# Layer-norm head of a fused attention and feed-forward kernel: loads on one queue, rstd on GpSimd, more normalising on ScalarE

## The chip, the cores and the metric

One core of a Trainium2 chip runs the whole program. The metric is the device time of one execution in microseconds, taken as the median of several runs. Engines are called PE (TensorE), DVE (VectorE), ACT (ScalarE), POOL (GpSimd) and SP (SyncE); PEld is PE's weight load.

## The reference, cut to what matters

```python
x = A_x                                   # (1, 2048, 576), bf16
xn = _layernorm(x, axis=-1)               # (x - mean) / sqrt(var + 1e-5)
return x + _A_ref(xn, A_wqkv, A_wo) + _B_ref(xn, B_w_gate, B_w_up, B_w_down)

# A: linear attention, 32 heads of 18
qkv = xn @ wqkv                           # phi(t) = where(t > 0, t + 1, exp(t)) + 1e-6
kv = einsum(phi(k), v); z = sum(phi(k))   # over the 2048 rows
o = (phi(q) @ kv) / (phi(q) . z + 1e-6); return o @ wo
# B: (gelu(xn @ w_gate) * (xn @ w_up)) @ w_down, hidden width 4608
```

The variance enters as rstd = (var + 1e-5) to the power -0.5, one number per row.

## The kernel before

The 2048 rows are 16 tiles of 128 (`NS`), the 576 columns of x five chunks of 128 (`KT`, the last one half full). The program has a first stage of some 57 us (layer norm, the k and q products, their activation phi, and an accumulated product of xn with phi(k) called G), a short passage to about 67 us, and then four rounds of the feed-forward part with the attention output added in.

Per tile n the first stage does this:

- statistics of the two halves of x (`ln_half`, L211, DVE) and their aggregate, mean and variance (`ln_aggr`, L214, DVE);
- rstd as exp(-0.5 ln(var + eps)), two one-column instructions on ACT (`ln_rstd`, L218 and L219);
- the normalised tile xn: on DVE (`ln_norm`, L232) for tiles 0 and 1, in two pieces each, and for even tiles after that; on ACT (`ln_norm_act`, L227) for odd tiles from 3 on, with a bias -mean*rstd made by POOL (`ln_bias`, L222);
- the transpose xnT: for tiles 0 and 1 by five PE transposes (L247) into PSUM and two copies (`tp_copy`, L251), for the others by a DMA transpose on SP's queue (L254);
- four groups of five matmuls, two halves of k and two of q (`kq_mm`, L262), each followed by an exp on ACT (L269) and a combining instruction on DVE (`kq_phi`, L274);
- seven matmuls of G (L293), which read xn and phi(k), and one POOL addition for z (`z_add`, L197).

The order on every engine is written out by a small planner. Each piece of work is a `step` with an engine, a length, a rank, the steps that it follows and, for loads, a time from which its data is taken to be there (`X_AT`, `W_AT`). `in_order` walks through the steps, takes the engine that can begin first and on it the lowest rank, and so makes one list; the instructions are issued in that list's order, and each engine runs its own in order. The lengths are the planner's reckoning only; waits at run time are on semaphores.

Ahead of the planned steps the loads are issued, in this order (`load_x` is L93, `load_w` L107 and L108; `load_w(1)` are the k weights, `load_w(0)` the q weights):

```python
load_x(0, 1)
load_x(1, 1, nc.scalar)
nc.scalar.preload_act_table_set("natural_log_exp_and_others")
load_w(1)
load_x(2, 2)
load_w(0)
load_x(4, 4)
```

PE meanwhile runs 38 matmuls on an identity (`spin`, L132), and POOL makes the identity and fills constant columns (L171 to L175), then the block mask `bmask` (L179 to L184), one chunk of `g_sb` (L189) and `ones` (L192). The mask is read when kv is masked, `g_sb` and `ones` in the passage after the first stage.

Of the kernel before, what the change touches and what calls it, by code (L numbers as in the profile page):

```python
# [8 lines left out]
ACT = mybir.ActivationFunctionType  # L9
ALU = mybir.AluOpType  # L10
BF16 = mybir.dt.bfloat16
F32 = mybir.dt.float32
# [3 lines left out]
P = 128  # L16
HP = 64
S = 2048
D = 576
H = 32  # L20
DH = 18
F = 4608
NS = S // P
# [5 lines left out]
KT = 5  # L29
# [4 lines left out]
EPS_LN = 1e-5  # L34
# [23 lines left out]
def kernel(  # L58
# [11 lines left out]
    nc = tc.nc  # L70
# [8 lines left out]
    const = ctx.enter_context(tc.tile_pool(name="const", bufs=1))  # L79
# [10 lines left out]
    x_sb = persist.tile([P, NS, D], BF16, name="x_sb")  # L90

    def load_x(n0, cnt, on=nc.sync):
        on.dma_start(x_sb[:, n0:n0 + cnt, :], x_view[:, n0:n0 + cnt, :])  # L93
# [14 lines left out]
        nc.sync.dma_start(wqkv_sb[0:HP, 4, c], A_wqkv[512:576, c])  # L108

    load_x(0, 1)  # L110
    load_x(1, 1, nc.scalar)
    nc.scalar.preload_act_table_set("natural_log_exp_and_others")
    load_w(1)
    load_x(2, 2)
# [4 lines left out]

    ident = const.tile([P, P], BF16, name="ident")  # L120
    make_identity(nc, ident[:])
    eps_ln = const.tile([P, 1], F32, name="eps_ln")
    nc.vector.memset(eps_ln[:], EPS_LN)
    eps_att = const.tile([P, 1], F32, name="eps_att")
    nc.vector.memset(eps_att[:], EPS_ATT)
    neg1 = const.tile([P, 1], F32, name="neg1")
    nc.vector.memset(neg1[:], -1.0)

    def spin(count):

        for _ in range(count):
            nc.tensor.matmul(ps_all[:, 7, 0:P], lhsT=ident[:], rhs=ident[:], start=True, stop=True)  # L132
# [19 lines left out]
    def load_gu(i, part):  # L152
# [17 lines left out]
    xn = apool.tile([P, NS, XW], BF16, name="xn")  # L170
# [4 lines left out]
    nc.gpsimd.memset(pk[:, :, D + 1:D + 2], 1.0)  # L175

    bmask = const.tile([P, CR], F32, name="bmask")
    bm3 = bmask[:].rearrange("p (h e) -> p h e", e=DH)
    nc.gpsimd.memset(bmask[:], 1.0)  # L179
    nc.gpsimd.affine_select(  # L180
        out=bm3, in_=bm3, compare_op=ALU.is_ge, fill=0.0,
        base=0, pattern=[[-DH, 7], [0, DH]], channel_multiplier=1,
    )
    nc.gpsimd.affine_select(  # L184
        out=bm3, in_=bm3, compare_op=ALU.is_ge, fill=0.0,
        base=DH - 1, pattern=[[DH, 7], [0, DH]], channel_multiplier=-1,
    )
    g_sb = apool.tile([P, KT, D], BF16, name="g_sb")
    nc.gpsimd.memset(g_sb[:, 4, :], 0.0)  # L189

    ones = const.tile([P, P], BF16, name="ones")
    nc.gpsimd.memset(ones[:], 1.0)  # L192
    z_sum = apool.tile([P, D], F32, name="z_sum")
    z_bf = apool.tile([P, D], BF16, name="z_bf")

# [6 lines left out]
    mv = persist.tile([P, NS, nc.vector.BN_AGGR_DIM], F32, name="mv")  # L202
    rstd = persist.tile([P, NS], F32, name="rstd")
    nbias = persist.tile([P, NS], F32, name="nbias")
# [3 lines left out]
    def ln_half(n, h):  # L208
        if h == 0:
            ln_raw[n] = asmall.tile([P, 2, nc.vector.BN_STATS_DIM], F32, name="stats")  # L210
        nc.vector.bn_stats(out=ln_raw[n][:, h, :], in_=x_sb[:, n, h * HALF:(h + 1) * HALF])  # L211

    def ln_aggr(n):
        nc.vector.bn_aggr(out=mv[:, n, :], in_=ln_raw[n][:])  # L214

    def ln_rstd(n):
        r = rstd[:, n:n + 1]
        nc.scalar.activation(out=r, in_=mv[:, n, 1:2], func=ACT.Ln, bias=eps_ln[:], scale=1.0)  # L218
        nc.scalar.activation(out=r, in_=r, func=ACT.Exp, scale=-0.5)  # L219

    def ln_bias(n):
        nc.gpsimd.tensor_scalar(  # L222
            out=nbias[:, n:n + 1], in0=mv[:, n, 0:1], scalar1=rstd[:, n:n + 1], scalar2=-1.0, op0=ALU.mult, op1=ALU.mult,
        )

    def ln_norm_act(n):
        nc.scalar.activation(  # L227
            out=xn[:, n, 0:D], in_=x_sb[:, n, :], func=ACT.Identity, bias=nbias[:, n:n + 1], scale=rstd[:, n:n + 1],
        )

    def ln_norm(n, c0=0, c1=D):
        nc.vector.tensor_scalar(  # L232
            out=xn[:, n, c0:c1], in0=x_sb[:, n, c0:c1], scalar1=mv[:, n, 0:1], scalar2=rstd[:, n:n + 1],
            op0=ALU.subtract, op1=ALU.mult,
        )
# [8 lines left out]
    def transposes(n, k0=0, k1=KT, b=None):  # L244
        b = TP_BANK[n] if b is None else b
        for kt in range(k0, k1):
            nc.tensor.transpose(tp_bank(b)[:, kt, :], xn[:, n, kt * P:(kt + 1) * P], ident[:])  # L247

    def tp_copy(n, k0=0, k1=KT, b=None, copy=acopy):
        b = TP_BANK[n] if b is None else b  # L250
        copy(out=xnT[:, k0:k1, n * P:(n + 1) * P], in_=tp_bank(b)[:, k0:k1, :])  # L251

    def dma_transposes(n):
        nc.sync.dma_start_transpose(xnT[:, :, n * P:(n + 1) * P], xn[:, n, 0:640])  # L254
# [4 lines left out]
    def kq_mm(n, which, hf):  # L259
        c = which * D + hf * HALF  # L260
        for kt in range(KT):
            nc.tensor.matmul(  # L262
                ps_all[:, KQ_BANK[which] + hf, :HALF], lhsT=xnT[:, kt, n * P:(n + 1) * P],
                rhs=wqkv_sb[:, kt, c:c + HALF], start=(kt == 0), stop=(kt == KT - 1),
            )
# [165 lines left out]
    def step(name, *args, **kw):  # L431
        steps[name] = _Step(*args, **kw)

    X_AT = [3.65, 4.20, 6.40, 6.40] + [9.50] * 4
    W_AT = {1: 5.50, 0: 7.60}

    for n0 in range(8, NS, 2):
        step(("x", n0), "SP", 0.50, n0 - 5.5, [], lambda n0=n0: load_x(n0, 2), ready=1.6 * n0 + 2.0, tail=3.0)
    for n in range(NS):
        lead = {0: -9.0, 1: 0.5, 2: -0.5, 3: -0.5}.get(n, 0.0)  # L440
        after_x = [("x", n // 2 * 2)] if n >= 8 else []
        x_at = X_AT[n] if n < 8 else 0.0
        for h in range(2):
            step(("stats", n, h), "DVE", 0.41, n - 2.2 + lead, after_x, lambda n=n, h=h: ln_half(n, h), ready=x_at)
        step(("aggr", n), "DVE", 0.21, n - 2.1 + lead, [("stats", n, 0), ("stats", n, 1)], lambda n=n: ln_aggr(n))
        step(("rstd", n), "ACT", 0.49, n - 2.1 + lead, [("aggr", n)], lambda n=n: ln_rstd(n))
        if n < TD:
            for i, (k0, k1, eng) in enumerate([(0, 3, "ACT"), (3, KT, "ACT" if n else "DVE")]):
                b = TP_BANK[n] - i
                step(("norm", n, i), "DVE", 0.25, n - 2.1 + lead, [("rstd", n)],  # L450
                     lambda n=n, k0=k0, k1=k1: ln_norm(n, k0 * P, min(k1 * P, D)))
                step(("tp", n, i), "PE", 0.20, n - 1.5 + lead, [("norm", n, i)],
                     lambda n=n, k0=k0, k1=k1, b=b: transposes(n, k0, k1, b))
                step(("xnT", n, i), eng, 0.30 if i else 0.48, n - 0.88 + lead, [("tp", n, i)],
                     lambda n=n, k0=k0, k1=k1, b=b, eng=eng: tp_copy(n, k0, k1, b, acopy if eng == "ACT" else vcopy))
            ready = [("xnT", n, 0), ("xnT", n, 1)]
        else:
            if n % 2:
                step(("bias", n), "POOL", 0.15, n - 2.1, [("rstd", n)], lambda n=n: ln_bias(n))
                step(("norm", n), "ACT", 0.65, n - 2.1, [("bias", n)], lambda n=n: ln_norm_act(n))  # L460
            else:
                step(("norm", n), "DVE", 0.43, n - 2.1, [("rstd", n)], lambda n=n: ln_norm(n))
            step(("xnT", n), "SP", 2.10, n - 1.9, [("norm", n)], lambda n=n: dma_transposes(n), tail=1.7)
            ready = [("xnT", n)]
        for which, rank in ((1, n), (0, n + 0.6)):
            for h in range(2):
                r = rank + h / 100
                free = [("phi", n - 1, which, h)] if n else []
                step(("mm", n, which, h), "PE", 0.615, r, ready + free, lambda n=n, w=which, h=h: kq_mm(n, w, h),
                     ready=W_AT[which], tail=0.15)  # L470
                step(("exp", n, which, h), "ACT", 0.49, r + 0.10, [("mm", n, which, h)],
                     lambda n=n, w=which, h=h: kq_exp(n, w, h))
                step(("phi", n, which, h), "DVE", 0.44, r + 0.15, [("exp", n, which, h)],
                     lambda n=n, w=which, h=h: kq_phi(n, w, h))
        if n > 0:
            idle = [("norm", n + 4) if n % 2 == 0 else ("bias", n + 4)] if n + 4 < NS else []
            step(("z", n), "POOL", 1.40, n + 2.0, [("phi", m, 1, h) for m in (0, n) for h in range(2)] + idle,
                 lambda n=n: z_add(n))
        step(("G", n), "PE", 0.75, n + 1.15, [("phi", n, 1, 0), ("phi", n, 1, 1)], lambda n=n: g_accumulate(n, G_A))
    step(("spin",), "PE", 0.11, -1.0, [("tp", 0, 1)], lambda: spin(2))  # L480

    def in_order(steps):

# [262 lines left out]
```

## Time and profile before

| | before |
|---|---|
| median of 3 runs | 512.57 us (512.55 to 512.60) |
| the profiled execution | 512.71 us |
| its span | 510.9 us |
| PE busy | 505.0 us, 99% |
| DVE, ACT, POOL busy | 41%, 27%, 5% |
| first stage, PE busy from 12 to 57 us | 45.0 of 45.0 us |
| ACT and DVE busy there | 35.9 and 36.0 us |

The span is what the profile covers; what lies around it makes up the rest of the execution's time. A row of the timeline gives start and length in us, engine, line, operation, output and inputs; in brackets stands how long the engine had been idle before, and what released it. The chain of waits gives start, length and the work that the end hung on in that time.

### The profile page before, as it was taken

What the parts mean: (1) busy time and instruction counts of PE and PEld (TensorE: products, weight loads), DVE (VectorE), ACT (ScalarE), POOL (GpSimd) and SP (SyncE); (2) the same over time, 40 slices, a digit from 0 to 9 for tenths busy, and PEclk for the clock granted to TensorE, in tenths of its full rate; (3) what the DMA queues carried; (4) which work ended last, traced back from release to release, by engine and by line L of the source; (5) the groups of instructions that cost most, each with busy time, mean ns of one, the idle gap of its engine ahead of it and who ended that gap; (6) DMA issues with size and microseconds to landing.
All of it is one profiled execution on the core that took longest, in us unless ns stands there. A gap on an engine that the chain in (4) does not pass through costs nothing.

```text
span 510.9 us, 10642 instructions
## 1 busy us (share of the span) xinstructions
PE 505.0 (99%) x4487; PEld 305.4 (60%) x4487; DVE 211.2 (41%) x447; ACT 136.8 (27%) x267; POOL 24.7 (5%) x38
## 2 busy tenths in 40 slices
PE   7999999999999999999999999999999999999997
PEld 6888854444587744444677644444777444445775
DVE  7887455555400045565200255555100356543100
ACT  5887533332310022332100023323000232232000
POOL 3344200000000000000000000000000000000000
PEclk9999999999999999999999999999999999999999
DMA  6643939999500067665300266567100565540000
GB/s 210 144 66 56 256 94 262 279 272 289 136 12 13 1 175 168 158 167 161 87 12 13 69 172 170 156 172 157 32 12 1 148 166 156 164 129 14 13 12 24
DMA packets 119002, 61.26 MB, mean 120 GB/s; under 512 B 25570, under 2 KB 118122, under 8 KB 118954
## 3 DMA queue, kind: packets, MB, share of 16 engines
q1 hardware_dynamic: 118810, 60.43, 45.3%
q8 instruction: 35, 0.57, 0.5%
q10 hardware_dynamic: 144, 0.15, 0.1%
q14 instruction: 13, 0.11, 0.1%
HBM read 52.86 MB, written 2.36 MB: 108 GB/s over the span
## 4 chain that ended last, share of the span: by engine, by line
PE 98%; DMA 1%; SPq 0%; DVE 0%; issue 0%
PE ps_all L324 55%; PE ps_all L668 28%; PE ps_all L262 7%; PE ps_all L293 3%; PE ps_all L673 3%; DMA wqkv_sb<-in_A_wqkv_dram 1%; PE ps_all L656 0%; PE ps_all L300 0%; PE ps_all L373 0%; PE ps_all L619 0%; SPq L93 0%; SPq L108 0%; DVE res L682 0%; SPq L107 0%; PE ps_all L361 0%
## 5 line engine op out<-in xcount | busy, mean ns | idle before, releaser
L324 PE MATMUL ps_all<-xnT,wg 64*128 64x512 bf16 x1152 | 271.9, 376 | 0.0
L324 PE MATMUL ps_all<-xnT,wu 64*128 64x512 bf16 x1152 | 271.5, 376 | 0.0
L608 ACT ACTIVATE gl<-ps_all 128x512 f32<-128x512 f32 x144 | 86.0, 597 | 311.1 <-PE ps_all L324 311.1
L609 DVE TENSOR_TENSOR hT<-ps_all,gl 128x512 bf16<-128x512 f32 x144 | 99.6, 691 | 131.2 <-ACT gl L608 130.7
L324 PEld LDWEIGHTS <-wu 64*128 64x128 bf16 x1152 | 108.3, 94 | 68.3
L324 PEld LDWEIGHTS <-wg 64*128 64x128 bf16 x1152 | 108.3, 94 | 67.7
L668 PE MATMUL ps_all<-wd_sb,hT 128*128 128x288 bf16 x1152 | 147.1, 286 | 0.0
L668 PEld LDWEIGHTS <-hT 128*128 128x128 bf16 x1152 | 112.3, 98 | 29.3 <-issue 1.2
L682 DVE TENSOR_TENSOR res<-ps_all,x_sb 128x288 bf16<-128x288 f32 x32 | 13.8, 455 | 146.4 <-PE ps_all L673 88.2
L324 PE MATMUL ps_all<-xnT,wr 64*128 64x512 bf16 x288 | 54.6, 376 | 0.0
L262 PE MATMUL ps_all<-wqkv_sb,xnT 128*128 128x288 bf16 x320 | 42.1, 286 | 0.5 <-ACT xnT L251 0.3
L262 PEld LDWEIGHTS <-xnT 128*128 128x128 bf16 x320 | 30.5, 98 | 7.9 <-ACT xnT L251 0.4
L269 ACT ACTIVATE phi_e<-ps_all,neg 128x288 f32<-128x288 f32 x64 | 30.9, 495 | 9.1 <-PE ps_all L262 6.3
L324 PEld LDWEIGHTS <-wr 64*128 64x128 bf16 x288 | 14.0, 94 | 16.8 <-issue 0.2
L673 PE MATMUL ps_all<-m_sb,pqT 128*128 128x288 bf16 x128 | 20.9, 286 | 0.0
L293 PE MATMUL ps_all<-hT,xn 128*128 128x288 bf16 (+4 forms) x144 | 18.8, 274 | 0.0
L274 DVE SCALAR_TENSOR_TENSOR pq<-phi_e,ps_all 128x288 bf16<-128x288 f32 x32 | 14.2, 449 | 7.7 <-ACT phi_e L269 7.4
L197 POOL TENSOR_TENSOR z_sum<-z_sum,hT 128x576 f32<-128x576 f32 x13 | 16.2, 1244 | 4.7 <-DVE hT L274 4.4
L293 PEld LDWEIGHTS <-xn 128*128 128x128 bf16 x144 | 14.0, 98 | 3.6 <-issue 0.2
L274 DVE SCALAR_TENSOR_TENSOR hT<-phi_e,ps_all 128x288 bf16<-128x288 f32 x32 | 14.1, 453 | 2.4 <-ACT phi_e L269 2.3
L673 PEld LDWEIGHTS <-pqT 128*128 128x128 bf16 x128 | 12.5, 98 | 3.2
L211 DVE BATCH_NORM_STATS2 stats<-x_sb 128x6 f32<-128x288 bf16 x32 | 13.6, 440 | 1.8 <-DMA x_sb<-in_A_x_dram 1.8
(62 smaller groups left out, 123.3 us busy)
## 6 DMA issues: line engine op xcount, KB each, us to landing
wg<-in_B_w_gate_dram SPq DMA_DIRECT2D x72, 256.0 KB, 2.9
wu<-in_B_w_up_dram SPq DMA_DIRECT2D x72, 256.0 KB, 3.5
wd_sb<-in_B_w_down_dram SPq DMA_DIRECT2D x12, 432.0 KB, 4.7
wr<-in_B_w_gate_dram SPq DMA_DIRECT2D x72, 32.0 KB, 2.8
wr<-in_B_w_up_dram SPq DMA_DIRECT2D x72, 32.0 KB, 3.0
out_dram<-res SPq DMA_DIRECT2D x15, 144.0 KB, 1.8
wqkv_sb<-in_A_wqkv_dram SPq DMA_DIRECT2D x3, 576.0 KB, 4.6
x_sb<-in_A_x_dram SPq DMA_DIRECT2D x5, 288.0 KB, 3.2
```

The costliest lines, as they stand in the source:

```text
L197: nc.gpsimd.tensor_tensor(out=z_bf[:] if n == NS - 1 else z_sum[:], in0=pk[:, 0, 1:D + 1] if n == 1 else z_sum[:], in1=pk[:, n, 1:D + 1], ...
L211: nc.vector.bn_stats(out=ln_raw[n][:, h, :], in_=x_sb[:, n, h * HALF:(h + 1) * HALF])
L262: nc.tensor.matmul(ps_all[:, KQ_BANK[which] + hf, :HALF], lhsT=xnT[:, kt, n * P:(n + 1) * P], rhs=wqkv_sb[:, kt, c:c + HALF], start=(kt == ...
L269: nc.scalar.activation(out=e[:], in_=ps_all[:, KQ_BANK[which] + hf, :HALF], func=ACT.Exp, bias=neg1[:], scale=1.0,)
L274: nc.vector.scalar_tensor_tensor(out=(pq, pk)[which][:, n, which + hf * HALF:which + (hf + 1) * HALF], in0=e_tiles[n, which, hf][:], scala ...
L293: nc.tensor.matmul(ps_all[:, b, col:col + w], lhsT=xn[:, n, kt * P:(kt + 1) * P], rhs=pk[:, n, 1 + d0:1 + d0 + w], start=(n == 0 and col = ...
L324: return nc.tensor.matmul(self.outs[i], lhsT=self.lhs(i, rows, kt), rhs=self.rhs(i, rows, kt), start=start, stop=stop, skip_group_check=True,)
L608: nc.scalar.activation(out=gl[:], in_=ps_all[:, b[0], :], func=ACT.Gelu_apprx_tanh)
L609: nc.vector.tensor_tensor(out=hT[:, GUB * k + i, :], in0=ps_all[:, b[1], :], in1=gl[:], op=ALU.mult)
L668: nc.tensor.matmul(self.acc(hf), lhsT=hT[:, f, j * P:(j + 1) * P], rhs=wd_sb[:, f, HALVES[hf]], start=(f == 0 and not paired), stop=False, ...
L673: nc.tensor.matmul(self.acc(hf), lhsT=pqT[:, c, self.ts], rhs=m_sb[:, c, HALVES[hf]], start=False, stop=(paired and c == 3), skip_group_ch ...
L682: nc.vector.tensor_tensor(out=self.res[:, hs], in0=self.acc(hf), in1=x_sb[:, self.n, hs], op=ALU.add)
```

## The change

- Tile 1 of x is loaded on SP's queue, right after tile 0, instead of on ACT's.
- rstd is made by POOL: an addition of eps and a power of -0.5, in place of Ln and Exp on ACT. The constant column `eps_ln` goes, a column `mhalf` of -0.5 comes.
- Which tiles ACT normalises is a string, `NORM`: D means DVE and A means ACT. Tile 1 goes to ACT (in two pieces, after a bias on POOL); of the later tiles 3, 5, 6, 7, 9, 10, 12, 13 and 15 are ACT's, nine where there were seven.
- `bmask`, the chunk of `g_sb` and `ones` become planned POOL steps after tile 2's rstd.
- The planner's lengths and times for the above are new, and with them the order: the five transposes of tile 1 now all stand before the q product of tile 0 (before, two of them stood inside it), and G of tile 1 stands before the k product of tile 2 (before, after it). The number of PE instructions is the same.

```diff
 load_x(0, 1)
-    load_x(1, 1, nc.scalar)
+    load_x(1, 1)
     nc.scalar.preload_act_table_set("natural_log_exp_and_others")
...
-    eps_ln = const.tile([P, 1], F32, name="eps_ln")
-    nc.vector.memset(eps_ln[:], EPS_LN)
+    mhalf = const.tile([P, 1], F32, name="mhalf")
+    nc.vector.memset(mhalf[:], -0.5)
...
     bmask = const.tile([P, CR], F32, name="bmask")
-    bm3 = bmask[:].rearrange("p (h e) -> p h e", e=DH)
-    nc.gpsimd.memset(bmask[:], 1.0)
...
+    def make_bmask():
+        bm3 = bmask[:].rearrange("p (h e) -> p h e", e=DH)
+        nc.gpsimd.memset(bmask[:], 1.0)
...
+    def clear_g():
+        nc.gpsimd.memset(g_sb[:, 4, :], 0.0)
+        nc.gpsimd.memset(ones[:], 1.0)
...
     def ln_rstd(n):
         r = rstd[:, n:n + 1]
-        nc.scalar.activation(out=r, in_=mv[:, n, 1:2], func=ACT.Ln, bias=eps_ln[:], scale=1.0)
-        nc.scalar.activation(out=r, in_=r, func=ACT.Exp, scale=-0.5)
+        nc.gpsimd.tensor_scalar_add(out=r, in0=mv[:, n, 1:2], scalar1=EPS_LN)
+        nc.gpsimd.tensor_tensor(out=r, in0=r, in1=mhalf[:], op=ALU.pow)
...
-    def ln_norm_act(n):
+    def ln_norm_act(n, c0=0, c1=D):
         nc.scalar.activation(
-            out=xn[:, n, 0:D], in_=x_sb[:, n, :], func=ACT.Identity, bias=nbias[:, n:n + 1], scale=rstd[:, n:n + 1],
+            out=xn[:, n, c0:c1], in_=x_sb[:, n, c0:c1], func=ACT.Identity, bias=nbias[:, n:n + 1], scale=rstd[:, n:n + 1],
         )
...
-    X_AT = [3.65, 4.20, 6.40, 6.40] + [9.50] * 4
-    W_AT = {1: 5.50, 0: 7.60}
+    NORM = "DADADAAADAADAADA"
+    COPY = ("DVE", "ACT")
+    POW = 0.55
+    X_AT = [3.05, 3.50, 6.40, 6.40] + [9.50] * 4
+    W_AT = {1: 5.60, 0: 8.00}
...
-        step(("rstd", n), "ACT", 0.49, n - 2.1 + lead, [("aggr", n)], lambda n=n: ln_rstd(n))
+        step(("rstd", n), "POOL", POW, n - 2.1 + lead, [("aggr", n)], lambda n=n: ln_rstd(n))
         if n < TD:
-            for i, (k0, k1, eng) in enumerate([(0, 3, "ACT"), (3, KT, "ACT" if n else "DVE")]):
+            for i, (k0, k1, eng) in enumerate([(0, 3, "ACT"), (3, KT, COPY[n])]):
                 b = TP_BANK[n] - i
-                step(("norm", n, i), "DVE", 0.25, n - 2.1 + lead, [("rstd", n)],
-                     lambda n=n, k0=k0, k1=k1: ln_norm(n, k0 * P, min(k1 * P, D)))
+                if NORM[n] == "A":
+                    if not i:
+                        step(("bias", n), "POOL", 0.15, n - 2.1 + lead, [("rstd", n)], lambda n=n: ln_bias(n))
+                    step(("norm", n, i), "ACT", (0.49, 0.36)[i], n - 2.1 + lead, [("bias", n)],
+                         lambda n=n, k0=k0, k1=k1: ln_norm_act(n, k0 * P, min(k1 * P, D)))
+                else:
+                    step(("norm", n, i), "DVE", (0.27, 0.20)[i], n - 2.1 + lead, [("rstd", n)],
+                         lambda n=n, k0=k0, k1=k1: ln_norm(n, k0 * P, min(k1 * P, D)))
...
-            if n % 2:
+            if NORM[n] == "A":
                 step(("bias", n), "POOL", 0.15, n - 2.1, [("rstd", n)], lambda n=n: ln_bias(n))
                 step(("norm", n), "ACT", 0.65, n - 2.1, [("bias", n)], lambda n=n: ln_norm_act(n))
...
-            idle = [("norm", n + 4) if n % 2 == 0 else ("bias", n + 4)] if n + 4 < NS else []
+            idle = [("norm" if NORM[n + 4] == "D" else "bias", n + 4)] if n + 4 < NS else []
...
+    step(("bmask",), "POOL", 0.95, 0.2, [("rstd", 2)], make_bmask)
+    step(("g",), "POOL", 0.75, 0.3, [("rstd", 2)], clear_g)
```

More of the change, by code (lines that the diff above doesn't have):

```diff
@@ L177 @@
     bmask = const.tile([P, CR], F32, name="bmask")
-    bm3 = bmask[:].rearrange("p (h e) -> p h e", e=DH)
-    nc.gpsimd.memset(bmask[:], 1.0)
[L180 to L187, printed above, removed]
     g_sb = apool.tile([P, KT, D], BF16, name="g_sb")
-    nc.gpsimd.memset(g_sb[:, 4, :], 0.0)
     ones = const.tile([P, P], BF16, name="ones")
-    nc.gpsimd.memset(ones[:], 1.0)
+    def make_bmask():
+        bm3 = bmask[:].rearrange("p (h e) -> p h e", e=DH)
+        nc.gpsimd.memset(bmask[:], 1.0)
+        nc.gpsimd.affine_select(
+            out=bm3, in_=bm3, compare_op=ALU.is_ge, fill=0.0,
+            base=0, pattern=[[-DH, 7], [0, DH]], channel_multiplier=1,
+        )
+        nc.gpsimd.affine_select(
+            out=bm3, in_=bm3, compare_op=ALU.is_ge, fill=0.0,
+            base=DH - 1, pattern=[[DH, 7], [0, DH]], channel_multiplier=-1,
+        )
+    def clear_g():
+        nc.gpsimd.memset(g_sb[:, 4, :], 0.0)
+        nc.gpsimd.memset(ones[:], 1.0)
     z_sum = apool.tile([P, D], F32, name="z_sum")
```

## The prediction

> **What bounds the kernel now.** I read the shares by engine first: PE is busy 99% of the span, so only PE's idle time and PE's order can pay. The chain of waits, cut to the first 16 us, says where PE is held (start, length, what):
>
> ```profile
> 0.81 0.39 SPq L93
> ...
> 1.25 0.42 SPq L107
> ...
> 2.95 5.56 DMA wqkv_sb<-in_A_wqkv_dram
> 8.50 0.04 issue
> 8.55 0.77 PE ps_all L262 x5
> 9.32 0.11 PE ps_all L247 x2
> 9.43 1.84 PE ps_all L262 x15
> 11.27 0.75 PE ps_all L293 x7
> 12.02 2.45 PE ps_all L262 x20
> ```
>
> The reader is to see that the path into the dense part is not the layer norm of the first tile but the second weight load (columns of q): issued at 2.95, landed at 8.50. From there PE runs without a gap, 3.20 us a tile (2.45 + 0.75), to the end of the stage. What happens before 8.55 costs only if it ends after 8.55. The timeline of that stretch:
>
> ```profile
> 3.73 0.82 DVE L211 BATCH_NORM_STATS2 stats<-x_sb 128x6 f32<-128x288 bf16 x2 [1.77 <-DMA x_sb<-in_A_x_dram]
> ...
> 4.83 0.30 ACT L218 ACTIVATE rstd<-mv,eps_ln 128x1 f32<-128x1 f32 x1 [2.31 <-DVE mv L214]
> 5.16 0.20 ACT L219 ACTIVATE rstd<-rstd 128x1 f32<-128x1 f32 x1
> ...
> 6.74 1.40 PE L262 MATMUL ps_all<-wqkv_sb,xnT 128*128 128x288 bf16 x10 [0.28 <-ACT xnT L251]
> ...
> 11.15 0.26 POOL L222 TENSOR_SCALAR nbias<-mv,rstd 128x1 f32<-128x1 f32 x1 [5.68 <-DVE pq L274]
> 11.45 0.87 ACT L227 ACTIVATE xn<-x_sb,nbias,rstd 128x576 bf16<-128x576 bf16 x1
> ```
>
> Tile 0's chain is x landed 3.71, statistics, rstd 5.36, transposes, k product 6.74 to 8.14. Then PE does three of tile 1's five transposes, waits 0.24 us for the weights, and slips the other two in at 9.32. The view by stretches shows the middle of the stage has room (columns: stretch, length, busy us of PE, PEld, DVE, ACT, POOL, clock, DMA share, GB/s):
>
> ```profile
> 12.00:57.00 45.00, 45.00 (x382) 36.52 (x380) 36.00 (x98) 35.90 (x88) 18.65 (x20) 1.00 0.53 114
> ```
>
> PE has no idle time there; DVE and ACT are at 80%, POOL at 41%. Relieving ACT in that stretch is worth nothing.
>
> **What the Trainium skill says.** "DMA: Bandwidth & Descriptors", Issuing engines are not separate DMA queues: loads from several engines interleave on the same 16 DMA engines and only issue time is saved. The trace agrees: the two first x tiles, issued at 0.80 by ACT and 0.81 by SP, land after 3.1 and 2.9 us, together. The same page, Queues, rings and completion order: each DMA engine alternates between the rings that have work; so a tile alone at the head of one ring should land earlier. "GPSIMD Engine Reference", 3.1: some 2.6 cycles an element for two inputs at 1.2 GHz, which makes 576 elements an estimated 1.25 us; the trace has 1.244 us (z_sum). Its section 2.1 also says that the first call into a freshly loaded library costs some 6 us that no instruction shows; the first POOL instructions here show no such gap. "ScalarE: Activation LUTs", What ACT_TABLE_LOAD costs, prices an ACTIVATE at 186 ns + 0.833 ns a column, 93 ns more for each operand that is a column of values, with 93 ns of overlap back to back: with scale and bias as columns 852 ns for 576, where the trace has 0.87 us. No page prices a power.
>
> **The change, part by part.** Times below are in the profile's clock.
>
> *x tile 1 from ACT's queue to SP's.* SP's issues of 0.4 to 0.6 us each (0.81, 1.25, 1.72, 2.33, 2.95) all move back by one, about 0.45 us: k weights from 1.25 to 1.70, q weights from 2.95 to 3.40. Tile 0 gets the DMA engines alone: 147 KB instead of 295 KB in front. By the stretches of 0.5 us (39, 76, 320, 341 GB/s from 1.5 on) 147 KB are through at 2.8 and 295 KB at 3.25; so it lands about 0.4 us earlier, I take 3.35 (3.2 to 3.7). The q weights are limited by bandwidth, not by issue: the DMA share is 1.0 or more and 313 to 408 GB/s in every half microsecond from 3.0 to 8.5, and the bytes ahead of them (1.9 MB) are unchanged. I take +0.05 us on their landing; bounds -0.1 and +0.45 (the whole shift of the issue).
>
> *rstd on POOL.* Two ACT instructions (0.30 + 0.20 us, 4.83 to 5.36) become an add and a power on POOL. The add is like nbias, 0.26 us; dependent POOL instructions start 0.07 apart (bmask, 4.07 to 4.47). The power appears in no row: not below 0.26 (nbias, the smallest arithmetic row there), and up to 1.24 (z_sum, 576 elements) as the other end. One element per partition should cost mostly dispatch: I take 0.35. POOL is free then: its memsets up to L175 end at 3.89, and the bmask and g_sb clears (1.9 us) move behind tile 2's rstd, where POOL was idle from 5.5 to 11.15; nobody needs them before 58. Walk: statistics 3.37 to 4.19, aggregate to 4.43, add 4.47 to 4.73, power 4.80 to 5.15, DVE norm from 5.19 (was 5.39), so k of tile 0 from about 6.5 to 7.95 (was 6.74 to 8.14).
>
> *Tile 1's norm on ACT.* On DVE the aggregate of tile 1 still stands behind tile 0's norm: 5.75 to 5.95. Then add, power and nbias on POOL, 6.0 to 7.0, and two ACT norms. The price above makes 384 and 192 columns an estimated 0.69 and 0.53 us, 0.09 of it overlapped: 7.02 to 8.15, and the last transposes end at 8.45. In the new order all five transposes stand before the q product, which the weights release at 8.55: this chain and the weights now end nearly together, with 0.1 us of slack. Stall taken: 0.05. Behind the norms on ACT wait tile 0's two exps (to about 9.15 instead of 8.87) and tile 1's copies (ending 9.95 instead of 9.84); PE wants the first copy at 9.8, it is there at 9.6, and the second 0.37 us later. No stall.
>
> *Transposes off the path.* The two at 9.32 go: -0.11 us.
>
> *The planner's new order.* G of tile 1 now comes before k of tile 2. Its second matmul needs phi of tile 1's second k half: exp behind the norm of tile 3 (0.87) ends near 12.75, phi near 13.25; PE arrives at 13.1. Stall 0.15 (0 to 0.3); before, G ran at 14.30.
>
> *More ACT norms, fewer DVE norms, no Ln and Exp, 16 rstd pairs on POOL.* ACT and DVE: nothing, PE is dense between 12 and 57. POOL per tile of 3.20 us: 1.24 + 0.26 + 0.35 + 0.17 for nbias, 2.0; rstd is wanted two tiles ahead. Nothing while the power stays under about 1.5.
>
> Sum: +0.05 + 0.05 - 0.11 + 0.15 = +0.14, rounded to +0.2 for the hand-over on semaphores from POOL. The profiled execution took 512.71 us (span 510.9), 0.14 over the median 512.57; there it would be 512.9, on the median **512.8**. A change of 0.2%, 1.03 us, is about what a measurement can tell from none.
>
> **Rivals.**
> 1. *The power is slow; slower.* Two powers lie in series before tile 1's transposes (tile 0's norm holds back tile 1's aggregate on DVE). The 0.1 us of slack is used up at a power of 0.4; each 0.1 us over that costs 0.2: net 0.09 + 2 x (P - 0.4). It decides over 1.03 us from P = 0.87; at the bound 1.24 it gives +1.8, 514.3. Beyond 1.5 POOL also falls behind PE tile by tile. For it: two dependent instructions where ACT took 0.53 together. Against: nbias at 0.26. A library load of 6 us at the first power belongs here (518); the built program shows no library instruction on POOL beyond those of before.
> 2. *The q weights come earlier; faster.* If they landed earlier, with the power at 0.26 and no wait at G, q would start at about 8.2: -0.35 - 0.11, 512.1, still no change to a measurement. Over 1.03 us would need some 15% more bandwidth than the trace ever shows there.
> 3. *The queue is issue-bound after all.* The full 0.45 us on the weights: 513.2.
> 4. *The head of the queue brings nothing:* first-packet latency, not sharing, sets 3.71. The chain ends 0.35 later, nearly all of it a stall now: 513.1.
>
> **How the numbers follow.** No measurable change (forecast with 2 to 4, all within 1.03): 0.78. Slower by more, rival 1: 0.19. Faster by more: 0.03. The range takes rival 2's end, 512.2, and rival 1 up to a power of about 1.07 us, 514.0; beyond lie some 0.12 above and 0.06 below.
>
> **What would show it.** In the profile after: x tile 0 landing near 3.35 and the first statistics there; the power's mean duration on POOL (0.3 to 0.4; over 0.87 I am wrong towards slower); the chain still running through the q weights near 8.5 and q starting at 8.55 to 8.7; a short PE wait for phi near 13; no PE wait between 14 and 57. If the chain instead runs through the norm of tile 1 on ACT and PE's first q product starts after 9.5, rival 1 is what happened; if q starts before 8.0, my bandwidth argument falls.

## The result, and the profile after

The changed kernel takes **515.5 us** (median of 4 runs, 514.67 to 515.82) against 512.56 us before on the same chip (512.35 to 512.60): a ratio of 1.0056 with a 95% interval of [1.0038, 1.0073], so slower by about 2.9 us. The profiled execution's span grew from 510.9 to 513.7 us. The forecast was 512.8, range 512.2 to 514.0.

The chain of waits after, first 16 us (start, length, what):

```profile
1.25 0.42 SPq L93
...
3.41 6.64 DMA wqkv_sb<-in_A_wqkv_dram
10.05 0.04 issue
10.09 2.61 PE ps_all L266 x20
12.70 0.75 PE ps_all L297 x7
13.45 1.23 PE ps_all L266 x10
14.68 0.75 PE ps_all L297 x7
```

The path is the same as before, through the q weights. They are issued 0.46 us later (3.41 for 2.95) but land 1.55 us later (10.05 for 8.50). The first G product (L297) starts at 12.70 instead of 11.27: 1.43 us are lost here. The timeline of that stretch after (start, length, engine, what, and in brackets the idle time before it with its releaser):

```profile
3.03 0.82 DVE L215 BATCH_NORM_STATS2 stats<-x_sb 128x6 f32<-128x288 bf16 x2 [1.08 <-DMA x_sb<-in_A_x_dram]
...
4.49 0.57 POOL L223 TENSOR_TENSOR rstd<-rstd,mhalf 128x1 f32<-128x1 f32 x1
5.10 0.62 DVE L236 TENSOR_SCALAR xn<-x_sb,mv,rstd 128x384 bf16<-128x384 bf16 x2 [0.32 <-POOL rstd L223]
...
6.61 1.40 PE L266 MATMUL ps_all<-wqkv_sb,xnT 128*128 128x288 bf16 x10 [0.18 <-ACT xnT L255]
...
7.20 1.15 ACT L231 ACTIVATE xn<-x_sb,nbias,rstd 128x384 bf16<-128x384 bf16 x2 [0.65 <-POOL nbias L226]
...
7.96 0.72 PE L251 MATMUL ps_all<-ident,xn 128*128 128x128 bf16 x5
...
10.09 2.61 PE L266 MATMUL ps_all<-wqkv_sb,xnT 128*128 128x288 bf16 x20 [1.40 <-DMA wqkv_sb<-in_A_wqkv_dram]
```

The layer norm did what the change says: statistics 0.7 us earlier than before, the k product at 6.61 instead of 6.74, all five transposes of tile 1 done near 8.7. PE then waits 1.40 us for the weights. The second loss is in the middle of the stage. The view by stretches, 12 to 57 us (PE, PEld, DVE, ACT, POOL busy):

```profile
12.00:57.00 45.00, 44.28 (x371) 35.52 (x370) 35.28 (x95) 32.10 (x64) 27.65 (x47) 1.00 0.51 111
```

PE was busy for all 45.00 us before and is no longer. Its G products start 3.20 us apart from 18.94 to 34.95, then at 38.71, 42.27 and 45.87, which is 0.56, 0.36 and 0.40 too late: 1.32 us; from there they are 3.20 apart again. With the 1.43 of the head that makes 2.75 of the span's 2.8. The timeline where the spacing breaks:

```profile
33.85 0.57 POOL L223 TENSOR_TENSOR rstd<-rstd,mhalf 128x1 f32<-128x1 f32 x1
34.39 1.29 POOL L201 TENSOR_TENSOR z_sum<-z_sum,hT 128x576 f32<-128x576 f32 x1
34.46 1.39 DVE L236 TENSOR_SCALAR xn<-x_sb,mv,rstd 128x576 bf16<-128x576 bf16 x1 [0.38 <-POOL rstd L223]
...
34.95 0.92 PE L297 MATMUL ps_all<-hT,xn 128*128 128x288 bf16 x7
...
35.77 0.81 DVE L278 SCALAR_TENSOR_TENSOR pq<-phi_e,ps_all 128x288 bf16<-128x288 f32 x2
36.26 2.61 PE L266 MATMUL ps_all<-wqkv_sb,xnT 128*128 128x288 bf16 x20 [0.40 <-DVE pq L278]
...
38.71 0.91 PE L297 MATMUL ps_all<-hT,xn 128*128 128x288 bf16 x7
...
39.14 0.87 ACT L231 ACTIVATE xn<-x_sb,nbias,rstd 128x576 bf16<-128x576 bf16 x1 [0.96 <-POOL nbias L226]
```

VectorE waits for a late rstd, so that its normalisation starts together with GpSimd's z_sum and takes 1.39 us instead of some 0.43; phi of q follows it, and PE waits for the bank that phi frees. Later ScalarE waits for nbias with its exponentials queued behind. GpSimd's groups after (last columns: busy, mean ns, idle before):

```profile
L223 POOL TENSOR_TENSOR rstd<-rstd,mhalf 128x1 f32<-128x1 f32 x16 | 9.1, 568 | 1.3
L222 POOL TENSOR_SCALAR rstd<-mv 128x1 f32<-128x1 f32 x16 | 3.6, 222 | 11.1 <-DVE mv L218 10.5
```

The pair takes 0.87 to 0.88 us with the gap between the two; the planner had been told 0.55 (`POW`).

### The profile page after: what moved, and what is told of

Same layout as the page of the kernel before. It is cut to its first block, busy times and chain, and to the rows that moved or that the text cites. A ratio compares the mean times of both kernels' runs of the same rounds, so it can differ in the third digit from the quotient of the medians.

```text
span 513.7 us, 10671 instructions
## 1 busy us (share of the span) xinstructions
PE 506.6 (99%) x4487; PEld 306.4 (60%) x4487; DVE 210.7 (41%) x443; ACT 133.5 (26%) x239; POOL 38.2 (7%) x73
## 4 chain that ended last, share of the span: by engine, by line
PE 93%; DVE 3%; DMA 1%; POOL 1%; issue 1%; ACT 1%; SPq 0%; ACTq 0%
PE ps_all L328 54%; PE ps_all L684 28%; PE ps_all L266 4%; PE ps_all L689 3%; PE ps_all L297 2%; DMA wqkv_sb<-in_A_wqkv_dram 1%; DVE pq L278 1%; DVE hT L278 1%; DVE stats L215 1%; ACT phi_e L273 1%; POOL z_sum L201 0%; PE ps_all L672 0%; PE ps_all L304 0%; DVE xn L236 0%; POOL rstd L223 0%
## 5 line engine op out<-in xcount | busy, mean ns | idle before, releaser
L297 PE MATMUL ps_all<-hT,xn 128*128 128x288 bf16 (+4 forms) x144 | 18.8, 274 | 0.0
L297 PEld LDWEIGHTS <-xn 128*128 128x128 bf16 x144 | 14.0, 98 | 3.6 <-issue 0.2
```

The costliest lines, as they stand in the source:

```text
L297: nc.tensor.matmul(ps_all[:, b, col:col + w], lhsT=xn[:, n, kt * P:(kt + 1) * P], rhs=pk[:, n, 1 + d0:1 + d0 + w], start=(n == 0 and col = ...
```

## The experiments

Each run's time stands beside the kernel before on the same chip. Two questions: why the q weights land so late, and what the middle loses.

**e1_x1_act: only the second x tile goes back to ScalarE's queue.**

```diff
-    load_x(1, 1)
+    load_x(1, 1, nc.scalar)
```

> The changed kernel with tile 1 of x back on ACT's queue; its order of instructions is otherwise the changed kernel's. Theory (the loads on one queue made the q weights late): they land near 8.5 to 8.7 again, not at 10.05. The first x tile then lands at 3.7 instead of 3.0, so the chain over POOL and ACT to tile 1's transposes ends near 9.35 and holds the first q product until then: 0.7 us earlier than in the changed kernel, about 514.7. Rival A (a slow DMA engine that has nothing to do with the queue): the weights land at 10 as before, 515.4. In both the 1.3 us lost between 35 and 46 us stay.

515.81 us, ratio 1.0063 [1.0051, 1.0076]: the time is not better than the changed kernel's. Yet the q weights land at 8.76 as the theory wanted, and the q product starts at 9.10. The timeline says where the gain of 1 us goes:

```profile
13.02 0.87 ACT L231 ACTIVATE xn<-x_sb,nbias,rstd 128x576 bf16<-128x576 bf16 x1 [1.38 <-POOL nbias L226]
...
14.81 0.79 PE L297 MATMUL ps_all<-hT,xn 128*128 128x289 bf16 x6 [0.85 <-DVE hT L278]
```

Tile 3's normalisation waits 1.38 us on ScalarE for nbias, and the exponential that G of tile 1 needs is queued behind it; PE waits 0.85 us inside that G. Followed back along the chain, nbias is late because VectorE's normalisation of tile 2 took 0.96 us beside GpSimd's clears, which put tile 3's statistics and its rstd back. In the changed kernel that normalisation began at 9.15 and kept its 0.43 us: x tile 0 had landed at 3.01 there and lands at 3.58 here, so the chain behind it ran earlier. What wait was left, the late q weights covered. So the load was shown to be the cause of the late weights, but moving it back does not by itself recover the time: it brings out a second delay.

**e2_x1_sp_only: the kernel before, with only this load moved to SP's queue.**

```diff
-    load_x(1, 1, nc.scalar)
+    load_x(1, 1)
```

> The kernel before with nothing changed but tile 1's load, moved from ACT's queue to SP's. Theory: the q weights land near 10.0 instead of 8.5, PE's first q product starts 1.4 to 1.5 us later, and the dense part follows: about 514.0. Rival A: 512.6, no change. Rival B (the bytes before the q weights are what counts): 512.6 too, weights at 8.5.

514.12 us, 1.0032 [1.002, 1.0044], as the theory said. The chain of waits of this run:

```profile
3.42 6.41 DMA wqkv_sb<-in_A_wqkv_dram
9.83 0.04 issue
9.88 0.77 PE ps_all L262 x5
```

One moved load, with ScalarE, GpSimd and VectorE as before, delays the q weights from 8.50 to 9.83, and no gap follows. That is the head's loss by itself.

**e3_true_costs: the changed kernel, the planner given the measured durations.**

```diff
-    POW = 0.55
+    POW = 0.90
...
-                step(("bias", n), "POOL", 0.15, n - 2.1, [("rstd", n)], lambda n=n: ln_bias(n))
-                step(("norm", n), "ACT", 0.65, n - 2.1, [("bias", n)], lambda n=n: ln_norm_act(n))
+                step(("bias", n), "POOL", 0.27, n - 2.1, [("rstd", n)], lambda n=n: ln_bias(n))
+                step(("norm", n), "ACT", 0.87, n - 2.1, [("bias", n)], lambda n=n: ln_norm_act(n))
```

Tile 1's nbias and half normalisations were given 0.27, 0.69 and 0.46 in the same way. Only the order of the instructions can differ.

> The changed kernel with the planner told the measured lengths: rstd on POOL 0.90 instead of 0.55, bias 0.27 instead of 0.15, ACT's norm 0.87 instead of 0.65 (halves 0.69 and 0.46). Only the order of instructions changes. Theory (the 1.3 us in the middle come from an order that reckons POOL too fast): PE runs without a gap from 16 to 57 us, 1.3 us less, about 514.1; the head stays late. Rival C (POOL is too slow in any order): the gaps move but stay, 515 or more.

513.95 us, 1.0027 [1.0016, 1.0038], as expected. The view by stretches:

```profile
12.00:57.00 45.00, 45.00 (x382) 36.51 (x380) 36.11 (x98) 34.00 (x66) 29.70 (x49) 1.00 0.63 135
```

PE is dense again with all the power instructions still on GpSimd, which is busy 29.70 of 45 us. The loss of the middle is one of order, not of load. The q weights still land at 10.14.

**e4_z_waits_norm: the changed kernel, where z_sum of tile n really waits for VectorE's normalisation of tile n + 4.** The planner only places it behind that step by its own clock.

```diff
+        if n + 4 in norm_ins:
+            tc.add_manual_dep(z.ins, norm_ins[n + 4].ins.name, SYNC, reason="z keeps off the norm")
```

> The changed kernel with one real wait more: POOL's addition z of tile n waits until DVE has normalised tile n+4, where DVE does that. Theory (the norm of tile 11, 1.39 us instead of 0.42, was held up because POOL's z addition began in the same moment): that norm takes 0.42 again, PE's gap near 36 us goes, and 0.5 to 1.0 of the 1.3 us in the middle come back, 514.4 to 514.9. Rival C (POOL simply runs late): the wait makes POOL later, 515.4 or more.

514.56 us, 1.004 [1.0027, 1.0052], inside the expected stretch. Two lines of its timeline:

```profile
34.85 0.43 DVE L240 TENSOR_SCALAR xn<-x_sb,mv,rstd 128x576 bf16<-128x576 bf16 x1 [0.37 <-POOL rstd L227]
...
42.87 2.61 PE L270 MATMUL ps_all<-wqkv_sb,xnT 128*128 128x288 bf16 x20 [0.24 <-DVE pq L282]
```

The normalisation still waits 0.37 us for its rstd, but takes 0.43 instead of 1.39. The G products of the middle lose 0.07 and 0.40 us, 0.47 where it was 1.32: about two thirds are recovered; ScalarE's waits for nbias are left. In this order of instructions the overlap with z_sum is the larger part of the loss.

**e5_x1_act_true_costs: e1 and e3 together.**

> The changed kernel with both repairs: tile 1's load back on ACT's queue, and the planner told POOL's and ACT's measured lengths. Sum of the two theories taken alone: 1.4 us in the head and 1.3 us in the middle come back, 512.6. Theory after the first runs (a second chain ends right behind the q weights: tile 2's norm on DVE beside POOL's clears, then rstd, bias and norm of tile 3 on POOL and ACT, with tile 1's exps behind them): PE's first q product starts at 9.1 instead of 10.1, but G of tile 1 waits some 0.8 us for phi as with the queue alone undone, so 513.7 to 514.0.

512.76 us over 14 runs, 1.0002 [0.9994, 1.001]: the kernel before, within what can be measured. The chain of waits:

```profile
7.23 1.40 PE ps_all L266 x10
8.63 0.28 PE ps_all L251 x5
8.91 2.45 PE ps_all L266 x20
11.36 0.75 PE ps_all L297 x7
```

PE is dense from here (45.00 of 45.00 in the middle stretch). The q weights land at 8.49, and now tile 1's transposes, at the end of GpSimd's chain, release the q product: G starts at 11.36, 0.09 later than before. The two causes together hold the whole slowdown; the rival's second chain, which was to cost over 1 us here, does not exist in the planner's new order.

**e6_rstd_act: the changed kernel with rstd by logarithm and exponential on ScalarE.** The planner is told so (0.49 us on ScalarE), so the order differs too; its figures for nbias and ScalarE's normalisations stay as they were.

```diff
-        nc.gpsimd.tensor_scalar_add(out=r, in0=mv[:, n, 1:2], scalar1=EPS_LN)
-        nc.gpsimd.tensor_tensor(out=r, in0=r, in1=mhalf[:], op=ALU.pow)
+        nc.scalar.activation(out=r, in_=mv[:, n, 1:2], func=ACT.Ln, bias=eps_ln[:], scale=1.0)
+        nc.scalar.activation(out=r, in_=r, func=ACT.Exp, scale=-0.5)
```

> The changed kernel with rstd computed by ScalarE again (logarithm and exponential), all else kept: loads on one queue, ScalarE's additional normalisations, the late clears. My theory (the middle part is lost because the planner gives GpSimd 0.55 us for an rstd that takes 0.86, so that GpSimd runs late): the head stays as late as in the changed kernel (q weights at about 10.0 us), TensorE has no gap between 15 and 46 us, GpSimd is busy about 9 us less, and the time is 514.0 us (512.56 + 1.43). Rival (ScalarE's additional normalisations are what makes the middle late): ScalarE now has the logarithms on top of them, the gaps stay or grow, 515.3 us or more.

514.12 us, 1.0028 [1.0017, 1.0039], as my theory said; the q weights land at 9.57. The view by stretches:

```profile
12.00:57.00 45.00, 44.87 (x378) 36.24 (x377) 35.89 (x97) 36.98 (x90) 19.23 (x22) 1.00 0.63 125
```

The 0.13 us short of 45.00 lie before 14; from there the timeline has PE at 3.20 us a tile throughout. ScalarE carries 36.98 us, more than in any other run, and holds nobody up. The added normalisations on ScalarE are not the cause. Nor are the planner's figures for them, which e3 changed together with the power's: here they are still wrong, and the middle is dense. No run changed the power's figure alone.

**e9_alternate: the changed kernel, normalisations divided evenly again.**

```diff
-    NORM = "DADADAAADAADAADA"
+    NORM = "DADADADADADADADA"
```

> The changed kernel with normalisations divided evenly again (VectorE and ScalarE in turn), rstd still on GpSimd at the planner's 0.55 us. My theory (GpSimd is late): two nbias fewer take 0.5 us off GpSimd, all the rest of its lateness stays, so gaps between 15 and 46 us stay in part, 514.6 to 515.6 us. Rival (the additional normalisations of ScalarE are the cause): no gaps, 514.0 us.

516.35 us, 1.0069 [1.0056, 1.0081]. Taking the additional normalisations off ScalarE does not help, and the time is even above the stretch that my theory gave. The timeline shows the same overlap in five normalisations, at 21.90, 28.01, 34.67, 40.75 and 46.35, of 0.98 to 1.30 us each:

```profile
34.67 1.07 DVE L236 TENSOR_SCALAR xn<-x_sb,mv,rstd 128x576 bf16<-128x576 bf16 x1
```

With every second tile on VectorE there are more normalisations that can meet a z_sum. Its head also lost 0.18 us to a G product waiting for phi; followed back, that chain runs to x tiles 2 and 3, which landed at 8.18 instead of 7.08.

**e7_x0_x1_one: the changed kernel, the first two x tiles as one transfer.**

```diff
-    load_x(0, 1)
-    load_x(1, 1)
+    load_x(0, 2)
```

> The changed kernel with tiles 0 and 1 loaded by one transfer on SP's queue, so that every later load is issued one step (0.45 us) earlier; still one queue. Theory D1 (the k weights arrive at an empty queue, so their first packets are slow: issue time is what counts): the rate stays above 300 GB/s from 3 to 4.5 us, few packets over 0.15 us, q weights land near 8.6; tile 0 lands near 3.4 to 3.7, the POOL chain holds the q product until 9.1 and G waits as when the queue alone is undone: 515.5. Theory D2 (one ring alone cannot keep the DMA engines busy, a second one is needed): the dip at 3 to 4.5 us and a landing near 10 stay, 515.5 to 516.

Here the question is why moving one load delays another by three times its issue. The view by half microseconds (last column GB/s), first of the kernel before, then of the changed one:

```profile
3.00:3.50 0.50, 0.50 (x7) 0.50 (x6) 0.00 (x0) 0.00 (x0) 0.50 (x1) 1.00 1.07 341
3.50:4.00 0.50, 0.50 (x8) 0.50 (x6) 0.27 (x1) 0.00 (x0) 0.44 (x4) 1.00 1.08 389
```

```profile
3.00:3.50 0.50, 0.50 (x7) 0.50 (x6) 0.47 (x2) 0.00 (x0) 0.50 (x1) 1.00 1.00 131
3.50:4.00 0.50, 0.50 (x8) 0.50 (x6) 0.47 (x2) 0.00 (x0) 0.33 (x3) 1.00 0.80 219
```

The DMA engines count as busy (share 1.00) and move a third of the bytes: single packets of 1152 bytes of the loads then under way take 200 to 600 ns there, where 51 ns is their median. e7 has no such dip:

```profile
3.00:3.50 0.50, 0.50 (x7) 0.50 (x6) 0.00 (x0) 0.00 (x0) 0.50 (x1) 1.00 1.01 330
```

Its q weights land at 8.79, though all loads are on one queue, so it is not the one queue alone that costs. (Its first load also goes in packets of 2304 bytes, where single tiles go in 1152.) Its time is 515.7 us all the same, 1.0058 [1.0046, 1.007]. The chain of waits says why:

```profile
7.36 2.58 PE ps_all L265 x10
9.95 0.53 PE ps_all L250 x5
10.48 2.68 PE ps_all L265 x20
```

The ten matmuls of the k product take 2.58 us instead of 1.40. The weights were there; PE itself was slow. The three entries take 5.79 us where e5's take 4.13. The trace tells why: its matmuls of 288 columns start 0.240 us apart until 10.75 and 0.122 apart after it, and its record of a full clock begins only at 10.81, where the changed kernel's begins at 6.25, ahead of its k product.

**e8_wk_second: the changed kernel, the k weights in second place, x tile 1 behind them.**

```diff
     load_x(0, 1)
-    load_x(1, 1)
     load_w(1)
+    load_x(1, 1)
     load_x(2, 2)
```

> The changed kernel with the k weights issued second on SP's queue, right after tile 0, and tile 1 after them. Theory D1: the k weights are issued at 1.25, before tile 0 has left the queue, and the slow first packets at 3 us go; the q weights, still issued at 3.4, land near 8.6. Theory D2: the dip stays and they land near 10. Tile 1 lands only with the k weights, near 5.3, so its norm is some 0.5 us later: a total of 515 to 516 either way; the landing and the rate at 3 to 4.5 us are what tells.

516.89 us, 1.0082 [1.0069, 1.0094]; the q weights land at 9.23, between the two expectations. The dip is there again, and earlier:

```profile
2.50:3.00 0.50, 0.50 (x8) 0.50 (x6) 0.00 (x0) 0.00 (x0) 0.47 (x1) 1.00 1.44 187
3.00:3.50 0.50, 0.50 (x7) 0.50 (x6) 0.44 (x2) 0.00 (x0) 0.50 (x1) 1.00 0.53 141
```

So the dip goes with the first weight load behind a lone x tile on a single queue, not with the place of x tile 1. The time is worse than the weights explain: x tile 1 lands at 6.11 and the k product starts at 8.21, and PE is slow in this run as well, 3.50 us for the twenty matmuls at 10.56, which take 2.45 in e5. Here the clock column (the third from the end) shows it, from 9.16 to 12.57:

```profile
9.50:10.00 0.50, 0.50 (x5) 0.24 (x3) 0.00 (x0) 0.50 (x2) 0.49 (x1) 0.50 0.12 46
```

**e10_clears_late: e5 with the clears of bmask, g_sb and ones behind z_sum of tile 11.**

```diff
-    step(("bmask",), "POOL", 0.95, 0.2, [("rstd", 2)], make_bmask)
-    step(("g",), "POOL", 0.75, 0.3, [("rstd", 2)], clear_g)
+    step(("bmask",), "POOL", 0.95, 12.0, [("z", 11)], make_bmask)
+    step(("g",), "POOL", 0.75, 12.1, [("z", 11)], clear_g)
```

> As the run with both repairs, and besides POOL's block mask, the clearing of g_sb and ones moved to the end of the first stage (after z of tile 11) instead of right after tile 2's rstd. Theory (these 1.7 us of POOL work stretch tile 2's norm on DVE and hold back tile 3's rstd): tile 2's norm takes 0.43 instead of 0.96 us, ACT's norm of tile 3 starts some 0.7 to 1.0 us earlier, G of tile 1 waits at most 0.2: 512.9 to 513.2. Rival (the chain is long by its own instructions): no change against the run with both repairs.

512.76 us, 1.0006 [0.9999, 1.0013], the same as e5, so the rival was right: in e5's order, where tile 2's normalisation takes 0.43 us beside them, the clears hold nobody up. They lengthen it in e1, e7 and e8 (0.96 to 1.16 us).

**e11_act_head: e5, with rstd of the first two tiles on ScalarE and their normalisation on VectorE, as in the kernel before.** **e12_act_head_wq** in addition issues the q weights ahead of x tiles 2 and 3 (and tells the planner so).

```diff
+        if n < TD:
+            nc.scalar.activation(out=r, in_=mv[:, n, 1:2], func=ACT.Ln, bias=eps_ln[:], scale=1.0)
+            nc.scalar.activation(out=r, in_=r, func=ACT.Exp, scale=-0.5)
+            return
...
-    NORM = "DADADAAADAADAADA"
+    NORM = "DDDADAAADAADAADA"
```

```diff
     load_w(1)
+    load_w(0)
     load_x(2, 2)
-    load_w(0)
     load_x(4, 4)
```

> Towards a version that beats both: the changed kernel with the second x tile on ScalarE's queue again, the planner given the measured durations, rstd and normalisation of the first two tiles as in the kernel before (logarithm and exponential on ScalarE, normalisation on VectorE), GpSimd's power for tiles 2 to 15 only. If the head was lost only to q weights and to the longer GpSimd chain, both are gone: q product at 8.50 to 8.60 us, first G product at 11.3, dense from there, 512.5 to 512.7 us. Rival: GpSimd gives rstd of tiles 2 and 3 too late and ScalarE's normalisation of tile 3 waits, so that a G product waits for phi: 513.0 us or more.

> As the run before, with the q weights issued ahead of x tiles 2 and 3. q weights land near 7.8 us (0.6 us of issue and 0.3 MB of x less ahead of them), the q product then waits only for the second tile's transposes at about 8.4: 0.1 us gained at most, 512.4 us. Rival: x tiles 2 and 3 land at 8.5 us instead of 6.5, their statistics and normalisation run beside the first exponentials, tile 2's G or its transposes come late, and the time is 512.9 us or more.

e11: 512.68 us over 13 runs, 1.0002 [0.9994, 1.0011]. Its span is 510.9, that of the kernel before to the tenth; its first G product starts at 11.13, 0.14 earlier than before, which no measurement of the time can tell. Its trace has a full overlap of a normalisation with z_sum too (38.65, 1.38 us), and PE has no gap behind it: an overlap does not cost by itself. e12: 515.0 us, 1.0044 [1.0031, 1.0057]. The rival was right there:

```profile
16.10 2.62 PE L272 MATMUL ps_all<-wqkv_sb,xnT 128*128 128x288 bf16 x20 [1.71 <-DMA xnT<-xn]
```

x tiles 2 and 3 land at 9.24, tile 2's transpose by DMA ends only at 16.05, and PE waits 1.71 us for it. No version of these beats the kernel before.

## Why the prediction was wrong, step by step

**The q weights' landing (the step "I take +0.05 us", bounds -0.1 and +0.45) failed.** It measured +1.55, beyond both bounds. I argued that the weights are limited by bandwidth and the bytes ahead of them are unchanged; that took the rate of the trace before, 313 to 408 GB/s, as a property of the chip. It belonged to an arrangement. In all seven runs where x tile 0 is alone ahead on SP and nothing comes on ScalarE's queue (the changed kernel, e2, e3, e4, e6, e8, e9), the rate between 3.0 and 3.5 us is 97 to 182 GB/s; in all seven others (before, e1, e5, e7, e10, e11, e12) it is 307 to 364. A second effect multiplies it: each load has 16 landing records in the trace, and PE is released by the last of them. In the trace's landing records the q weights' shares arrive between 7.61 and 8.50 us before, and between 7.95 and 10.05 after: the first is 0.34 late, the last 1.55. The shares fell behind by unequal amounts: the first one of x tiles 4 to 7 lands at 9.84, before the q weights are complete. Rival 3, the issue-bound queue, had the sign but only 0.45 of it; none of the four rivals was what happened. Why packets are slow in just that arrangement was not settled: e7 and e8 show that it is neither the single queue alone nor x tile 1, but not what it is. (The 1.9 MB that the prediction counts ahead of the q weights include these themselves, 0.66 MB, and its clears of 1.9 us are 1.7 by their rows; neither is what failed.)

**"Nothing while the power stays under about 1.5" failed.** GpSimd's sum of 2.0 us a tile was a little low with the power at 0.57, but e3 shows that the load fits in. The step compared an average with the period, where what counts is when each result is due: the planner's order assumed 0.55 us for 0.87, so rstd came late (VectorE waits 0.38 us for it at 34.46), and z_sum, kept off VectorE's normalisation only by that clock, met it. Cost +1.32. My sentence that no PE wait would show between 14 and 57 was wrong with it. I had read the planner's figure in the diff and bounded the power without asking what the order does if the figure is wrong.

**The power, 0.35 estimated, is 0.57.** Inside its bounds, and below the 0.87 from which rival 1 was to decide. Rival 1's mechanism is real, and small: in e5, where the weights are on time, the chain through GpSimd releases the q product, and G starts 0.09 us later than before, though x tile 0 lands later there (3.80) than in the changed kernel. The order differs too, so this is no clean measure of the formula.

**What held.** The walk of the layer norm: tile 0's normalisation at 5.10 (5.19 predicted), k product 6.61 (6.5), tile 1's normalisations 7.20 to 8.35 (7.02 to 8.15), transposes done near 8.7 (8.45). In part this was luck: x tile 0 landed 0.34 us earlier than the 3.35 of the forecast, and the power took 0.22 us longer than its 0.35; for tile 0 the two nearly cancel. ScalarE's halves took 0.706 and 0.532 us, estimated at 0.69 and 0.53 by the price in the Trainium skill's "ScalarE: Activation LUTs", What ACT_TABLE_LOAD costs. That a tile alone at the head lands earlier held, and by more than I took, with the landing at 3.01, under the range of 3.2 to 3.7, so rival 4 is out. That this brings nothing held as well: the chain through the weights decides. **The wait of 0.15 at G of tile 1** did not show in the changed kernel, where the q product came late; in e1, with the weights early and x tile 0 later, it was 0.85, since I had not seen that VectorE's normalisation of tile 2 can lengthen beside GpSimd's clears.

## What to carry to other kernels

An order planned from durations is only as good as those durations: when an operation moves to another engine, measure it and give the planner the figure before judging the move (here that alone was worth 1.5 us). A transfer rate read from a trace holds for that arrangement of the queues; if the head of a queue is rearranged, take the landing of every load behind it as unknown. And where a second delay lies close behind the first, or the repair itself moves another chain, repairing one shows no gain: repair both before calling either harmless.

## What the runs showed of the hardware

- A VectorE normalisation of 128x576 bf16 takes 0.43 us alone and up to 1.39 us when a GpSimd addition has just begun (1.39 in the changed kernel, 1.07 in e9's line above; 0.43 in e4, where the addition is made to wait). Where the normalisation began first, it kept its length (0.42 us at 44.79 in the changed kernel, z_sum from 44.95). The Trainium skill's "SBUF — State Buffer", SBUF: two separate sides, says that a GpSimd operation and certain VectorE ones hold a shared pair of ports exclusively, for a whole instruction, and the second blocks. The trace agrees in kind: z_sum started 0.07 us ahead of it, at 34.39, and kept its usual length (1.29 us). The normalisation ended 0.17 us after z_sum did, less than its own 0.43, so by these times it was not blocked for all of it.
- A power of one column on GpSimd is 0.568 us, more than twice the addition of a constant (0.222) or nbias (0.264).
- In e7 and e8 PE ran at half its rate for a while: matmuls of 288 columns start 0.240 us apart, otherwise 0.122. In e7 this ends at 10.81, where the trace's clock records begin (in the other runs they begin between 4.23 and 6.85, ahead of the k product); the clock column prints 1.00 where there is no record, so its 1.00 before that is no measurement. In e8 the records give the full clock from 5.74, half of it from 9.16 and the full one from 12.57, and the spacing of the matmuls follows. The Trainium skill's "TensorE: Matmul & The Clock Gate", What's actually happening, describes a clock that is halved at first and after a window in which PE was idle, and is full after a busy one. The traces agree in kind: in the kernel before the matmuls of the spin start 0.107 us apart until 4.25, where its records begin, and 0.056 apart after; in e8 PE stood idle for 1.66 us, up to 7.30, in the stretch before the clock fell, and the half clock lasted 3.41 us. No run tested that idle time is the cause.
